# Deriving the feature map's derivative again in the backward instead of storing it, with a new order of the forward

## The chip, the core and the metric

The program runs on one core of one Trainium2 chip, in one launch. The metric is the device time of an execution in microseconds, the median of several. Before the change it is 2144.93 us (three runs, 2142.76 to 2145.81).

## The reference

Four attention blocks in a row over 2048 tokens of width 640 (32 heads of 20): a linear one (A), a sliding one (B, window 256), A and B again with the same weights; then the gradients of the result with respect to the input and the four weight matrices. All in bf16. The part that the change touches is the feature map phi of the linear block:

```python
x = x + _A_ref(_layernorm(x, axis=-1), A_wqkv, A_wo)
x = x + _B_ref(_layernorm(x, axis=-1), B_wqkv, B_wo)
...
phi = lambda t: jnp.where(t > 0, t + 1, jnp.exp(t)) + 1e-6
pq, pk = phi(q), phi(k)
kv = jnp.einsum("bhsd,bhse->bhde", pk, v)
z = jnp.einsum("bhsd->bhd", pk)
num = jnp.einsum("bhqd,bhde->bhqe", pq, kv)
den = jnp.einsum("bhqd,bhd->bhq", pq, z)[..., None] + 1e-6
```

Its derivative is 1 for t > 0 and exp(t) otherwise, that is min(exp(t), 1). Since phi is max(t, 0) + min(exp(t), 1) + 1e-6, the same derivative is also min(phi - 1e-6, 1).

## The kernel before

The tokens are cut into 16 tiles of 128. The layers have the numbers 0 (A), 1 (B), 2 (A), 3 (B). The span runs through five parts:

- a first pass over the tiles for layer 0 (`a_first`): layer norm, q, k and v, the feature map;
- a joined pass (`ab_pass(0)`) that finishes layer 0, does layer 1, and begins layer 2 (its k and v alone);
- a joined pass (`ab_pass(2)`) that finishes layer 2 and does layer 3, with the start of the backward;
- the sliding backward of layer 3 (`B_attn_bwd`), then a backward phase `bwd_phase(3, 2, 1)` for the projections of layer 3 and the linear block of layer 2;
- the same again for layers 1 and 0, `bwd_phase(1, 0, None)`, at the end of the span.

In the forward, q and k of a tile come out of PE in halves of 320 columns (`a_qkv`, line 488). For each half ACT writes the exponential into a buffer `ee` (line 516), DVE takes the minimum with 1 in place (line 517), and DVE adds max(t, 1e-6) to it and so writes phi (line 520), for q into `pp`, for k into the persistent `gcar`. Line 467 copies transposes of q's phi to `pqT` on ACT, and line 501 copies half of v out of PSUM on ACT in layer 0. ACT's queue then issues the stores of a tile (line 416): `pq` and `pk`, the feature maps, `eq` and `ek`, the derivatives, and `v`. `ee` is a ring of four buffers, and a buffer is free again when its store has landed. Layer 2's queries are done later, from the layer norm kept in `pqT` (`late_q`, line 542): for the first `EARLY` tiles as fillers between the two joined passes, for the others inside `ab_pass(2)`; matmuls are line 553, and `pq` and `eq` are stored from there.

In the second half of a backward phase `lin_grads` (line 1465) does a tile of the linear block's gradients. Its `start` flips dNT, pkT and vT by DMA transposes and loads `eq` and `ek` on SP's queue (line 1128), into rings of two buffers each. Six chunks follow; for q and k DVE multiplies what PE has summed by `eq` or `ek` (line 1503). `tail` (line 1276) then carries the result through the projection: ACT copies dh (line 1309), DVE forms a product and its sum (line 1317), ACT scales (1324), POOL adds the gradient so far (1327), DVE updates it (1329). In the first backward phase `local_dO` follows on the updated gradient: transposes, a projection, a product on POOL (1377), a reduction on DVE (1380), two small instructions on DVE (1382, 1384) and a store issued on ACT's queue (1387).

The order on each engine comes from a planner (`Sched`). Program code makes instructions in an order that the numbers in `AT` set for the forward: each is a position in tiles, relative to a tile's number, at which a step's items are put (`num`, `out`, `outb`, `qkv`, `lag`, `af` and so on). The planner then walks the engines by estimated durations and picks on each the ready instruction that can start first, and among these the one made first. PE may take an instruction at most `AHEAD` places ahead of the first one not yet taken. DMAs are estimated too, on one channel, so a DMA that goes changes the estimated times of what follows. Each engine executes its list in order.

Of the kernel before, what the change touches and what calls it, by code (L numbers as in the profile page):

```python
# [18 lines left out]
HPAD = 32  # L19
WIN = 256  # L20
LN_EPS = 1e-5
AHEAD = 19
IDLE = 300


# [177 lines left out]
class Kern:  # L203
    def __init__(self, ctx, tc, x0, A_wqkv, A_wo, B_wqkv, B_wo, grad_out, outs):
# [68 lines left out]
        for l in (0, 2):  # L273
            self.sv[l] = dict(
                pq=d.tile([T, D], BF, name=f"pq{l}"), pk=d.tile([T, D], BF, name=f"pk{l}"),
                eq=d.tile([T, D], BF, name=f"eq{l}"), ek=d.tile([T, D], BF, name=f"ek{l}"),
                v=d.tile([T, D], BF, name=f"v{l}"), o=d.tile([T, D], BF, name=f"o{l}"),
                r32=d.tile([T, self.H], F32, name=f"r32{l}"),
                mbd=d.tile([D, D + P], BF, name=f"mbd{l}"),
            )  # L280
# [53 lines left out]
    def forward(self, slabs):  # L334
# [5 lines left out]
        with ExitStack() as st:  # L340
# [147 lines left out]
            def a_qkv(l, tt, hnT):  # L488
# [3 lines left out]
                def chunk(ci):  # L492
                    def f():
# [27 lines left out]
                            out=pd(), in0=ps.t[:, 0:CW], scalar=1e-6, in1=es(), op0=ALU.max,  # L521
                            op1=ALU.add), [ps, (e, ci)], [(c["p"], ci) if kind == "q" else ("pk", tt, ci)])
                        if ci == 3 and "q" in c:
                            p_, e = c["p"], c["q"]
                            turn("s", lambda: pqT[:, :, tt * P:(tt + 1) * P], lambda: p_.t, DT, [(p_, 0), (p_, 1)],
                                 [("pqT", tt)])
                            dma("ACT", lambda: self.tm_view(sv["pq"])[:, tt, :], lambda: p_.t, 160 * KB,
                                [(p_, 0), (p_, 1)], [])
                            dma("ACT", lambda e=e: self.tm_view(sv["eq"])[:, tt, :], lambda e=e: e.t, 160 * KB,
                                [(e, 0), (e, 1)], [])  # L530
                        if ci == 3:
                            e = c["k"]
                            dma("ACT", lambda: self.tm_view(sv["pk"])[:, tt, :], lambda: pk[:, tt, :], 160 * KB,
                                [("pk", tt, 2), ("pk", tt, 3)], [])
                            dma("ACT", lambda e=e: self.tm_view(sv["ek"])[:, tt, :], lambda e=e: e.t, 160 * KB,
                                [(e, 2), (e, 3)], [])
                    return f
                return [chunk(ci) for ci in range(6)]

# [2 lines left out]
            def late_q(l, tt, where="s1", **F):  # L542

                sv = self.sv[l]
                q_left.discard(tt)
                e, p_ = R["ee"].buf(), R["pp"].buf()
                own = lambda: pqT[:, :, tt * P:(tt + 1) * P]
                for ci in range(2):
                    ps, c0 = R[where].buf(), ci * CW
                    for k0, k1 in ((0, 2), (2, DT)):  # L550
                        def f(ps=ps, c0=c0, k0=k0, k1=k1):
                            for k in range(k0, k1):
                                nc.tensor.matmul(ps.t[:, 0:CW], lhsT=own()[:, k, :], rhs=wsb["Wqkv_A"][:, k, c0:c0 + CW],
                                                 start=(k == 0), stop=(k == DT - 1))
                        op("PE", pe([CW] * (k1 - k0)), f, [("pqT", tt), ("Wqkv_A", ci)], [ps], **F)
                    es = lambda c0=c0: e.t[:, c0:c0 + CW]
                    op("ACT", av(CW), lambda ps=ps, es=es: nc.scalar.activation(es(), ps.t[:, 0:CW], ACT.Exp), [ps],
                       [(e, ci)], **F)
                    op("DVE", v4(CW), lambda es=es: nc.vector.tensor_scalar(out=es(), in0=es(), scalar1=1.0, scalar2=None,
                                                                            op0=ALU.min), [], [(e, ci)], **F)  # L560
                    op("DVE", vp(CW), lambda ps=ps, es=es, c0=c0: nc.vector.scalar_tensor_tensor(
                        out=p_.t[:, c0:c0 + CW], in0=ps.t[:, 0:CW], scalar=1e-6, in1=es(), op0=ALU.max, op1=ALU.add),
                       [ps, (e, ci)], [(p_, ci)], **F)
                if tt < 2:
                    turn("mm", own, lambda: p_.t, DT, [(p_, 0), (p_, 1)], [("pqT", tt)])
                else:
                    flip(own, lambda: p_.t, 160 * KB, [(p_, 0), (p_, 1)], [("pqT", tt)], **F)
                dma("ACT", lambda: self.tm_view(sv["pq"])[:, tt, :], lambda: p_.t, 160 * KB, [(p_, 0), (p_, 1)], [], **F)
                dma("ACT", lambda: self.tm_view(sv["eq"])[:, tt, :], lambda: e.t, 160 * KB, [(e, 0), (e, 1)], [], **F)

            def a_kv(l):
                sv = self.sv[l]
# [390 lines left out]
            def a_first(items, l, base, lag=0.0, late=()):  # L963


                for tt in range(TT):
# [10 lines left out]
                        return lambda: cell["fs"][i]()  # L977
                    spread(items, base + tt + 0.9 + lag, base + tt + 1.9 + lag, [g(i) for i in range(6)][2 * (tt in late):])

            EARLY = 6  # L980
            AT = {0: dict(num=-2.458, out=-1.707, outb=1.792, step=0.144, qkv=-0.99, wide=0.745, lag=0.42, af=2.042, al=-0.11),
                  2: dict(lq=-3.207, num=-2.403, out=-1.76, outb=1.696, step=0.086, qkv=-0.985, wide=0.584, lag=0.35, gT=0.745, dO=1.691, dOs=0.137)}

            def ab_pass(l, last):
                a = AT[l]
# [105 lines left out]
    def bwd_phase(self, lb, la, nb, ahead, raw):  # L1091
# [9 lines left out]
        with ExitStack() as st:  # L1101
# [363 lines left out]
            def lin_grads(tt, items, t0):  # L1465
# [4 lines left out]
                def start():  # L1470
                    for nm, src, size in (("dNT", self.tmp_dN, 192 * KB), ("pkT", sv["pk"], 160 * KB),
# [1 line left out]
                        c[nm] = b = R[nm].buf()  # L1473
                        flip(lambda b=b: b.t, lambda src=src: src[row, :], size,
                             [("dNd", tt)] if nm == "dNT" else [], [b])
                    c["eq"], c["ek"] = load("eq", sv["eq"], tt), load("ek", sv["ek"], tt)

                def chunk(kind, ci):
                    def f():
# [413 lines left out]
```

## Time and profile before

| | |
|---|---|
| median of the runs | 2144.93 us |
| the profiled execution, its own time | 2145.22 us |
| its span, first to last instruction | 2143.5 us |
| PE busy in the span | 2008.2 us, 94% |
| DVE busy | 1440.1 us, 67% |
| ACT busy | 1203.3 us, 56% |
| POOL busy | 879.4 us, 41% |
| mean granted TensorE clock | 0.975 |
| q and k exponentials of the first pass (line 516) | 12.9 to 115.8 us |
| products with eq and ek (line 1503), first phase | 1218.4 to 1359.0 us |
| the same, last phase | up to 2066.7 us |

A row of engine instructions gives the start and the duration in us, the engine, the line, what it writes and reads with partitions x elements, and in brackets how long the engine sat idle before it and what ended that. A row of stretches gives the busy us of PE, its weight loads, DVE, ACT and POOL with the number of instructions in brackets, the granted clock, the share of the DMA engines and GB/s. Rows with ACTq or SPq are DMA issues on an engine's queue; they aren't in the busy time. A row of one line's instructions has its count, and minimum, median and maximum in ns. A row that groups has, behind the bar, the busy us and the mean ns of one, then the idle time before them.

### The profile page before, as it was taken

How to read it: one execution, taken by the hardware profiler on the slowest of the kernel's cores; microseconds unless marked ns; L12 is line 12 of the kernel's file. 1: busy time of each engine (PE TensorE's matmuls, PEld its weight loads, DVE VectorE, ACT ScalarE, POOL GpSimd, SP SyncE). 2: the span in 40 equal slices, each digit the busy share in tenths (PEclk: the TensorE clock that was granted, in tenths of full speed). 3: DMA queues.
4: the chain of work that ended last, by engine and by line, in shares of the span. 5: the costliest groups of instructions: out<-in, count | busy, mean ns of one | idle time of the engine just before them, and what ended most of it. 6: DMA issues, size and time to landing. Idle time of an engine off the chain costs nothing. (4 is left out here: it accounts for less than half of the span.)

```text
span 2143.5 us, 68024 instructions
## 1 busy us (share of the span) xinstructions
PE 2008.2 (94%) x27908; PEld 1389.2 (65%) x27908; DVE 1440.1 (67%) x2954; ACT 1203.3 (56%) x1995; POOL 879.4 (41%) x1850
## 2 busy tenths in 40 slices
PE   6879999889999899999899999999999999999999
PEld 4656666656666577777666667656777765666764
DVE  6757777567776599999634368606998984444651
ACT  3527878647888589899422233216988881221430
POOL 1015666316777456666223223204665652230210
PEclk9989999999999899999899999999999999999999
DMA  9928989469998788987987899847999998989943
GB/s 291 256 106 179 191 193 191 119 198 201 210 208 191 146 157 151 161 161 155 193 185 168 213 200 203 175 104 142 157 158 151 170 170 162 199 185 227 186 111 102
DMA packets 943687, 376.43 MB, mean 176 GB/s; under 512 B 821776, under 2 KB 923664, under 8 KB 943120
## 3 DMA queue, kind: packets, MB, share of 16 engines
q1 hardware_dynamic: 866176, 299.16, 71.9%
q10 hardware_dynamic: 77200, 72.94, 11.1%
q8 instruction: 218, 3.57, 0.7%
q14 instruction: 93, 0.76, 0.1%
HBM read 109.02 MB, written 112.07 MB: 103 GB/s over the span
## 5 line engine op out<-in xcount | busy, mean ns | idle before, releaser
L1693 DVE TENSOR_TENSOR ds_sb<-pair,e_sb 128x768 bf16<-128x768 f32 x480 | 437.6, 951 | 57.8 <-PE pair L1654 49.6
L1673 ACT ACTIVATE e_sb<-pair 128x768 bf16<-128x768 f32 x480 | 390.9, 815 | 95.6 <-PE pair L1654 67.4
L839 POOL TENSOR_SCALAR_AFFINE_SELECT e_sb<-e_sb 128x384 bf16<-128x384 bf16 (+1 forms) x512 | 198.3, 406 | 357.5 <-ACT e_sb L830 335.7
L830 ACT ACTIVATE e_sb<-s_ps 128x1152 bf16<-128x1152 f32 (+2 forms) x256 | 273.8, 1070 | 100.2 <-PE s_ps L826 78.4
L1685 POOL TENSOR_SCALAR_AFFINE_SELECT e_sb<-e_sb 128x256 bf16<-128x256 bf16 x448 | 182.0, 406 | 227.1 <-ACT e_sb L1673 226.9
L1327 POOL TENSOR_TENSOR gw<-w,gcar 128x640 f32<-128x640 f32 x64 | 89.4, 1397 | 423.4 <-ACT w L1324 406.8
L1138 PEld LDWEIGHTS <-slabR 128*128 128x128 bf16 x1920 | 185.6, 98 | 116.1 <-DMA slabR<-o 3.7
L1682 POOL TENSOR_SCALAR_AFFINE_SELECT e_sb<-e_sb 128x256 bf16<-128x256 bf16 x512 | 206.5, 406 | 89.3 <-ACT e_sb L1673 89.3
L1718 PEld LDWEIGHTS <-dsT 128*128 128x128 bf16 x2880 | 146.2, 97 | 97.7 <-issue 91.5
L1709 ACT COPY dsT<-dsT_ps 128x768 bf16<-128x768 bf16 x240 | 191.2, 796 | 9.4 <-PE dsT_ps L1706 6.6
L448 PE MATMUL mm_ps<-slabR,hnTB 128*128 128x320 bf16 x960 | 170.5, 308 | 10.5 <-DVE gcar L520 6.0
L1706 PE MATMUL dsT_ps<-ident,ds_sb 128*128 128x128 bf16 x1848 | 158.2, 223 | 1.3 <-ACT dsT L1709 1.1
L1722 PEld LDWEIGHTS <-ds_sb 128*128 128x128 bf16 x2880 | 145.1, 96 | 0.8 <-issue 0.8
L1722 PEld LDWEIGHTS <-e_sb 128*128 128x128 bf16 x2880 | 145.0, 96 | 0.0
L844 POOL TENSOR_SCALAR_AFFINE_SELECT e_sb<-e_sb 128x512 bf16<-128x512 bf16 x224 | 142.6, 636 | 0.0
L833 ACT ACTIVATE e_sb<-s_ps 128x384 bf16<-128x384 f32 (+2 forms) x256 | 119.9, 468 | 32.3 <-PE s_ps L826 15.1
L1138 PE MATMUL dw_ps<-dqkv,slabR 128*128 128x480 bf16 x640 | 134.7, 366 | 0.0
L1309 ACT ACTIVATE dh<-mm_ps 128x320 f32<-128x320 f32 x64 | 28.0, 437 | 189.8 <-PE mm_ps L1138 164.9
L1138 PE MATMUL dw_ps<-dqkv,om 128*128 128x480 bf16 x640 | 134.2, 366 | 0.0
L1654 PE MATMUL pair<-slabR 32*128 32x384 bf16 (+2 forms) x1024 | 120.5, 326 | 12.0 <-DVE ds_sb L1693 5.2
L1138 PEld LDWEIGHTS <-om 128*128 128x128 bf16 x800 | 77.5, 98 | 71.3 <-DMA om<-o 2.4
L864 PEld LDWEIGHTS <-e_sb 128*128 128x128 bf16 x2880 | 105.5, 96 | 26.6 <-POOL e_sb L844 7.5
(234 smaller groups left out, 4357.6 us busy)
## 6 DMA issues: line engine op xcount, KB each, us to landing
qkvp<-qk_slab SPq DMA_DIRECT2D x64, 256.0 KB, 3.7
hn<-slabR SPq DMA_DIRECT2D x64, 160.0 KB, 2.9
qkvp<-v_slab SPq DMA_DIRECT2D x32, 256.0 KB, 3.4
slabR<-qkvp SPq DMA_DIRECT2D x16, 512.0 KB, 4.8
o<-o SPq DMA_DIRECT2D x48, 160.0 KB, 2.9
eq<-ee ACTq DMA_DIRECT2D x32, 160.0 KB, 3.0
pq<-pp ACTq DMA_DIRECT2D x32, 160.0 KB, 2.4
ek<-ee ACTq DMA_DIRECT2D x32, 160.0 KB, 2.7
```

The lines of the kernel that those rows point to most:

```text
L448: nc.tensor.matmul(ps.t[:, w0:w0 + width], lhsT=lhsT(), rhs=rhs(), start=start, stop=stop)
L830: op("ACT", av(3 * nkt * P), lambda: nc.scalar.activation(e.t[:, 0:3, 0:nkt, :], s3.t[:, :, 0:nkt * P].rearrange("p h (i q) -> p h i q", q=P),
L839: nc.gpsimd.affine_select(out=v, in_=v, compare_op=ALU.is_ge, fill=0.0, base=0, pattern=[[0, h1 - h0], [1, P]], channel_multiplier=-1)
L1138: nc.tensor.matmul(ps.t[:, w0:w0 + width], lhsT=lhsT(), rhs=rhs(), start=start, stop=stop)
L1673: nc.scalar.activation(E[n][:, 2 * p:2 * p + 2], PR[h][:, :, 0:3 * P].rearrange("p i (j q) -> p i j q", q=P), ACT.Exp, scale=self.c_att)
L1682: nc.gpsimd.affine_select(out=e[:, :, j, :], in_=e[:, :, j, :], compare_op=ALU.is_ge, fill=0.0, base=0, pattern=[[0, 2], [-1, P]], channel ...
L1685: nc.gpsimd.affine_select(out=e[:, :, j, :], in_=e[:, :, j, :], compare_op=ALU.is_ge, fill=0.0, base=-1, pattern=[[0, 2], [1, P]], channel ...
L1693: nc.vector.tensor_mul(DS[n][:, hs], PR.pop(h)[:, :, 0:3 * P].rearrange("p i (j q) -> p i j q", q=P), E[n][:, hs])
L1706: nc.tensor.transpose(ps[:, i, j, :], DS[n][:, 2 * p + i, j, :], self.ident)
L1709: (nc.scalar.copy if by == "A" else nc.vector.tensor_copy)(TSB[h], TPS.pop(h))
L1718: nc.tensor.matmul(a[:, 0, hh, :], lhsT=TSB[2 * n + hh // 2][:, hh % 2, j, :], rhs=ld[g]["K"][:, k, cs], start=(i == 0), stop=(i == len(dq ...
L1722: nc.tensor.matmul(a[:, 1 + x, hh, :], lhsT=src[n][:, hh, j, :], rhs=ld[g][rhs][:, q, cs], start=(i == 0), stop=(i == len(dkv) - 1))
```

## The change

The forward keeps `ee` on chip only for phi and stores neither `eq` nor `ek`: 64 stores of 160 KB less on ACT's queue, from two places in `a_qkv` and one in `late_q`, and four DRAM tensors less. The backward loads `pq` and `pk` into the same buffers as it loaded `eq` and `ek`, and DVE takes min(x - 1e-6, 1) in place, in one instruction behind each load. The numbers of the forward change: `AHEAD`, `EARLY`, and all of `AT`.

```diff
-AHEAD = 19
+AHEAD = 18
...
-                eq=d.tile([T, D], BF, name=f"eq{l}"), ek=d.tile([T, D], BF, name=f"ek{l}"),
...
                         if ci == 3 and "q" in c:
-                            p_, e = c["p"], c["q"]
+                            p_ = c["p"]
...
-                            dma("ACT", lambda e=e: self.tm_view(sv["eq"])[:, tt, :], lambda e=e: e.t, 160 * KB,
-                                [(e, 0), (e, 1)], [])
                         if ci == 3:
-                            e = c["k"]
...
-                            dma("ACT", lambda e=e: self.tm_view(sv["ek"])[:, tt, :], lambda e=e: e.t, 160 * KB,
-                                [(e, 2), (e, 3)], [])
...
-                dma("ACT", lambda: self.tm_view(sv["eq"])[:, tt, :], lambda: e.t, 160 * KB, [(e, 0), (e, 1)], [], **F)
...
-            EARLY = 6
-            AT = {0: dict(num=-2.458, out=-1.707, outb=1.792, step=0.144, qkv=-0.99, wide=0.745, lag=0.42, af=2.042, al=-0.11),
-                  2: dict(lq=-3.207, num=-2.403, out=-1.76, outb=1.696, step=0.086, qkv=-0.985, wide=0.584, lag=0.35, gT=0.745, dO=1.691, dOs=0.137)}
+            EARLY = 8
+            AT = {0: dict(num=-2.329, out=-1.53, outb=1.773, step=0.003, qkv=-0.851, wide=0.713, lag=0.391, af=2.216, al=-0.231),
+                  2: dict(lq=-3.14, num=-2.341, out=-1.768, outb=1.691, step=0.084, qkv=-0.988, wide=0.634, lag=0.313, gT=0.79, dO=1.598, dOs=0.307)}
...
-                    c["eq"], c["ek"] = load("eq", sv["eq"], tt), load("ek", sv["ek"], tt)
+                    for nm, p_ in (("eq", "pq"), ("ek", "pk")):
+                        c[nm] = b = load(nm, sv[p_], tt)
+                        op("DVE", 310, lambda b=b: nc.vector.tensor_scalar(
+                            out=b.t, in0=b.t, scalar1=-1e-6, scalar2=1.0, op0=ALU.add, op1=ALU.min), [], [b])
```

## The prediction

> **What bounds the kernel now.** I read first the page, then stretches of 50 us, then the instructions around what the change removes and adds.
>
> ```profile
> span 2143.5 us, 68024 instructions
> ```
>
> ```profile
> core 0: us, PE busy (x) PEld busy (x) DVE busy (x) ACT busy (x) POOL busy (x), PEclk, DMA share, GB/s
> ...
> 50.00:100.00 50.00, 43.39 (x394) 31.73 (x393) 37.73 (x108) 30.83 (x76) 0.00 (x0) 1.00 0.98 254
> ...
> 200.00:250.00 50.00, 47.49 (x821) 33.51 (x820) 38.64 (x97) 40.95 (x67) 32.94 (x73) 1.00 0.88 180
> ...
> 550.00:600.00 50.00, 49.11 (x851) 34.60 (x849) 39.40 (x98) 41.27 (x63) 37.70 (x78) 1.00 1.05 220
> ...
> 1300.00:1350.00 50.00, 47.26 (x440) 35.99 (x439) 44.46 (x96) 15.80 (x42) 16.19 (x12) 1.00 1.06 209
> ...
> 2000.00:2050.00 50.00, 50.00 (x510) 39.49 (x508) 35.90 (x87) 21.19 (x54) 11.18 (x8) 1.00 0.88 179
> ```
>
> Five stages matter. In the first pass over the tiles (row at 50 us) no engine is full and the DMA share is 0.98. In the two passes that join a linear and a sliding layer (200 and 550 us) PE is busy 95 and 98 per cent. In the second half of the first backward phase (1300 us) PE is at 95 and DVE at 89 per cent: the two wait for each other. In the same half of the last phase (2000 us) PE is never idle and DVE has 14.1 of 50 us free. Busy time leaves out the issuing of DMAs, and this is where the first pass is decided:
>
> ```profile
> L416 ACTq DMA_DIRECT2D eq<-ee x32: 326/422/1445, 15.0 to 654.7; - x32
> L416 ACTq DMA_DIRECT2D pq<-pp x32: 326/332/628, 15.5 to 654.4; - x32
> L416 ACTq DMA_DIRECT2D ek<-ee x32: 326/388/672, 23.6 to 422.8; - x32
> L416 ACTq DMA_DIRECT2D pk<-gcar x32: 339/345/1209, 25.5 to 423.3; - x32
> L416 ACTq DMA_DIRECT2D v<-vv x32: 338/363/972, 25.9 to 424.8; - x32
> ```
>
> These are the five stores of a tile (minimum, median, maximum ns): by their medians 0.422 + 0.332 + 0.388 + 0.345 + 0.363 = 1.85 us of ACT's queue. The period of a tile comes from the copy of a half of v, of which these are the first and the eleventh in a steady row:
>
> ```profile
> 53.47 0.42 ACT L501 CAST vv<-s_ps 128x320 bf16<-128x320 f32 x1 [0.47 <-PE s_ps L448]
> ...
> 113.28 0.42 ACT L501 CAST vv<-s_ps 128x320 bf16<-128x320 f32 x1 [0.98 <-DVE vv L504]
> ```
>
> (113.28 - 53.47) / 10 = 5.98 us. The 50 us of the row then hold 8.36 tiles, so a tile takes 5.19 us of PE, 4.51 of DVE and 3.69 of ACT; with the issues ACT's queue is taken for 5.54 of 5.98 us. One tile shows the harm:
>
> ```profile
> 68.45 0.69 ACT L467 COPY pqT<-s_ps 128x640 bf16<-128x640 bf16 x1
> 68.45 0.99 ACTq L416 DMA_DIRECT2D eq<-ee  x1
> ...
> 69.54 0.39 ACTq L416 DMA_DIRECT2D ek<-ee  x1
> ...
> 69.97 0.42 ACT L501 CAST vv<-s_ps 128x320 bf16<-128x320 f32 x1 [0.83 <-PE mm_ps L448]
> ...
> 70.44 0.84 PE L448 MATMUL s_ps<-Wqkv_A,hnTA 128*128 128x320 bf16 x5 [0.68 <-ACT vv L501]
> ```
>
> The copy starts 0.04 us after ek's issue has ended, 0.83 us after ACT's last work, and PE stands 0.68 us until it has its bank back.
>
> **The change part by part.** *Stores in the first pass.* eq and ek of 16 tiles go, 0.81 us of the queue per tile. The gain lies between nothing (another engine sets the same period) and 16 x (5.98 - 5.19) = 12.6 us, where PE sets it. I take the store that stands right ahead of the copy, ek: 16 x 0.388 = **6.2 us gained**.
>
> *Stores in the two joined passes.* There go 16 of ek (layer 2's keys) and 16 of eq (its queries, recomputed late): 16 x 0.388 + 16 x 0.422 = 13.0 us of ACT's queue. But there ACT waits for PE:
>
> ```profile
> ACT e_sb L830 <- PE s_ps L826: 46.0, 55, 12.7
> ```
>
> 46.0 us in 55 waits between 120 and 420 us. Between 0 and 13.0 I take a quarter, **3 us gained**.
>
> *EARLY from 6 to 8.* Two more tiles' late queries run as fillers between the passes and not inside the second one. The row groups the matmuls of the ten tiles that run inside it; the second row is where the fillers go:
>
> ```profile
> L553 PE MATMUL mm_ps<-Wqkv_A,pqT 128*128 128x320 bf16 x100 | 16.7, 298 | 0.0
> ```
>
> ```profile
> 440.00:450.00 10.00, 8.05 (x85) 5.82 (x82) 7.53 (x22) 4.96 (x10) 0.00 (x0) 1.00 1.06 268
> ```
>
> A tile takes 1.67 us of PE; two leave a stage with PE at 98 per cent for one with 1.95 of 10 us free. Between 3.3 us gained and 3.3 lost (the fillers delay the sums that the next pass waits for), I take **2 us gained**.
>
> *New positions and AHEAD 18.* They change the order of the same instructions. Nothing in the rows prices an order. PE is idle 2.51 of 50 us at 200 us, so over some 410 us of joined passes 20 us; I let a quarter of that, 5 us, go either way and take **0**.
>
> *Recomputation.* Each backward phase now reads pq and pk where it read eq and ek: as many loads on SP, of the same size, with no queue moved. Behind each load stands one DVE instruction, in place on 128x640 bf16; 64 in all. Its duration isn't in the trace. The same operation on half the length and another on the same length:
>
> ```profile
> L517 DVE TENSOR_SCALAR ee<-ee x96: 225/234/686, 13.4 to 422.5; 128x320 bf16<-128x320 bf16 x96
> ```
>
> ```profile
> L482 DVE TENSOR_SCALAR slabR<-x,mv,rs x64: 430/446/774, 9.3 to 678.6; 128x640 bf16<-128x640 bf16 x64
> ```
>
> Between 0.234 and 0.446 I take the middle, 0.34 us: 0.68 per tile, 10.9 us in a phase of 16 tiles. The instruction also waits for its load, of which this is the row of the DMA issues (KB, median us to landing):
>
> ```profile
> eq<-eq SPq DMA_DIRECT2D x32, 160.0 KB, 3.4
> ```
>
> Behind the waiting instruction would stand all of DVE's evacuations and behind these PE. The loads are issued about a tile ahead (two buffers), so I price this wait at nothing; without that lead it is up to 3.4 us for a load.
>
> In the last phase the work goes into DVE's free time: a tile's 0.68 against 14.1 us per 50. PE covers it without a gap, so **0**; with the cover gone it would be 10.9. In the first phase there is a closed chain:
>
> ```profile
> 1293.64 1.34 POOL L1377 TENSOR_TENSOR prod<-slab,o 128x640 f32<-128x640 bf16 x1
> 1293.72 1.95 DVE L1329 SCALAR_TENSOR_TENSOR gcar<-slabR,sm,gw 128x640 bf16<-128x640 bf16 x1 [0.35 <-POOL gw L1327]
> ...
> 1295.99 0.80 DVE L1380 TENSOR_REDUCE dd<-prod 128x32 f32<-128x640 f32 x1
> ...
> 1297.10 0.30 DVE L1384 SCALAR_TENSOR_TENSOR slab<-dd,slab 128x32 bf16<-128x32 f32 x1
> ...
> 1297.43 0.37 ACTq L1128 DMA_DIRECT2D dOpt<-slab  x1
> ...
> 1297.85 0.44 ACT L1309 ACTIVATE dh<-dw_ps 128x320 f32<-128x320 f32 x1 [2.01 <-DVE dqkv L1503]
> ...
> 1298.41 0.82 DVE L1317 CUSTOM_DVE_ANT_0 scr<-dh,slabR 128x640 bf16<-128x640 f32 x1 [0.30 <-ACT dh L1309]
> ...
> 1299.49 0.92 ACT L1324 ACTIVATE w<-dh,sm,rs 128x640 f32<-128x640 f32 x1 [0.18 <-DVE sm L1323]
> ...
> 1300.49 1.40 POOL L1327 TENSOR_TENSOR gw<-w,gcar 128x640 f32<-128x640 f32 x1 [5.50 <-ACT w L1324]
> ...
> 1301.92 1.95 DVE L1329 SCALAR_TENSOR_TENSOR gcar<-slabR,sm,gw 128x640 bf16<-128x640 bf16 x1 [0.35 <-POOL gw L1327]
> ```
>
> From the gradient's update on DVE through the reduction, ACT's store, ACT's copy, DVE's product, ACT, POOL and back to the update: 1301.92 - 1293.72 = 8.20 us, the period of a tile. (ACT's copy of dh names a product on DVE as its releaser, but starts 0.05 us after the store's issue has ended, and that issue stands ahead of it in ACT's queue.) DVE waits twice in it, 0.30 and 0.35 us. A new instruction put into one of these gaps costs next to nothing; one put between the update and the store lengthens the chain by all of its 0.34. Between 0 and 16 x 0.68 = 10.9 us I take half, **5.4 us lost**; the update, and with it the transposes on PE that read it, are then what comes late.
>
> The sum: -6.2 - 3 - 2 + 0 + 5.4 = -5.8 us. The profiled execution took 2145.22 us (1.7 outside its span); that gives 2139.4. It stands 0.3 above the median of the runs, 2144.93, so the forecast is **2139.1 us**.
>
> **The rivals.** *The chain in the first backward phase takes it back.* If both instructions stand between the update and the store, the whole 10.9 us counts. There is more: an instruction of this kind is held while POOL works.
>
> ```profile
> 273.17 0.63 POOL L844 TENSOR_SCALAR_AFFINE_SELECT e_sb<-e_sb 128x512 bf16<-128x512 bf16 x1
> 273.21 0.69 DVE L517 TENSOR_SCALAR ee<-ee 128x320 bf16<-128x320 bf16 x1 [1.36 <-ACT ee L516]
> ```
>
> POOL ends at 273.80, DVE's instruction at 273.90, after 0.69 us where its median is 0.234. In the chain POOL works for 2.74 of 8.20 us. With half of the 32 instructions held for 0.45 us (0.686 - 0.234) it is 7.2 us more. Forward's 11.2 us gained, 18.1 lost: 2145.2 + 6.9, less 0.3, is 2151.8 us, slower. It decides once the period exceeds 8.20 + 11.2 / 16 = 8.9 us. For it speaks DVE's 89 per cent, against it the two gaps, which hold 0.65 of the 0.68.
>
> The Trainium skill, SBUF — State Buffer, "Who interferes with whom", states the same as a rule: a DVE instruction in a two-port mode and a GpSimd instruction exclude each other, whoever comes second waits until the first has ended. By that rule alone a new instruction that comes just behind POOL's sum waits for nearly all of it, three times the hold that I priced; the pair above agrees with it.
>
> *What goes is hidden anyway.* The five stores are only what ACT does while PE is busy, the period of the first pass stays near PE's and DVE's own chain, and the backward's work lies in its gaps: forward gains 2, the backward loses 2, 2144.9 us. For it speaks that many of ACT's waits in the first pass name PE; against it, that PE waited for ACT in the tile shown.
>
> *The whole bound comes.* First pass 12.6, half of 13.0 in the joined passes, 3.3 from EARLY, nothing lost behind: -22.4, 2122.5 us. It asks that PE run without a gap from the first tile on, while at 50 us it still loses 6.6 of 50.
>
> **How the numbers follow.** About 0.2 per cent, 4.3 us, is what a measurement tells from no change. The forecast gets 0.45 (own range 2131 to 2145: 0.33 of it faster, 0.12 within the bound), the lengthened chain 0.23 (0.21 slower, 0.02 within), the hidden work 0.20 (0.16 within, 0.02 to each side), the whole bound 0.12. Faster 0.47, same 0.30, slower 0.23. The range 2127 to 2154 leaves out most of the whole bound's case and the tail of the lengthened chain.
>
> **What would show it.** In the first pass the eq and ek issues are gone and the copy of v follows ACT's last work; the period falls from 5.98 to about 5.6 us. The second joined pass has eight instead of ten late tiles. In the first backward phase the update's period grows from 8.20 to about 8.5 us, and the new instruction takes 0.3 to 0.4 us, more where POOL runs. In the last phase PE stays without a gap. The prediction is wrong if the first pass keeps its period, if the chain's period passes 8.9 us, if DVE stands waiting for pq or pk, or if the new order opens gaps in the joined passes.

## The result and the profile after

The changed kernel takes **2125.76 us** (median of 4 runs, 2123.76 to 2129.68), the kernel before, run beside it, 2143.85 us (4 runs, 2141.27 to 2145.81). The ratio is 0.9923, 95% interval 0.9909 to 0.9937: 16.5 us by the ratio. The forecast was 2139.1 us. The sign was right, but the gain is about three times the 5.8 us forecast. The median of the runs lies 1.2 us below the range of 2127 to 2154 us; the ratio applied to 2144.93 us, from which the forecast started, gives 2128.4, just inside it.

The line of the page with the span, after:

```profile
span 2122.0 us, 67891 instructions
```

The two profiled spans are 21.5 us apart (2143.5 and 2122.0). Landmarks, read from the first or last row of a line in each trace, cut the difference up (us):

| stretch | before | after | difference |
|---|---|---|---|
| start to the last copy of v on ACT (first pass) | 117.8 | 104.4 | -13.4 |
| from there to the last exponential of layer 2's keys (first joined pass) | 304.0 | 296.2 | -7.8 |
| from there to the first product of layer 3's sliding backward (second joined pass, seams) | 316.8 | 312.8 | -4.0 |
| first to last product of that sliding backward | 307.1 | 310.0 | +2.9 |
| first to last update of the gradient, first backward phase | 318.1 | 318.3 | +0.2 |
| the sliding backward of layer 1 | 307.9 | 306.0 | -1.9 |
| first to last update of the last phase | 295.0 | 296.9 | +1.9 |
| all seams and the end | 176.8 | 177.4 | +0.6 |

The whole gain lies in the forward, and more than half of it in the first pass. The two rows of the sliding backward are code that the change does not touch; over all kernels of this study the first of them took 305.4 to 314.3 us, so a difference of 2 or 3 us in one stretch of one profile means nothing by itself.

Part of the 21.5 us is not the change. PE is idle for 135.3 us of the span before and 119.0 after, 16.3 us less; the other 5.2 us are shorter busy time (2008.2 and 2003.0 us) for the same number of matmul records (27908). The mean granted TensorE clock was 0.975 in the one profile and 0.981 in the other, and it varies between executions of one kernel (0.976 to 0.983 in 31 runs of the kernel before). The 16.3 us agree with the 16.5 of the ratio. By the first three rows of the table PE's idle time falls by 10.6, 7.5 and 1.3 us, and in the rest of the span it grows by 3.1.

The same five stretches of 50 us as in the prediction, after (columns as there: busy us of PE, its weight loads, DVE, ACT, POOL with counts, granted clock, DMA share, GB/s):

```profile
core 0: us, PE busy (x) PEld busy (x) DVE busy (x) ACT busy (x) POOL busy (x), PEclk, DMA share, GB/s
50.00:100.00 50.00, 48.54 (x461) 36.26 (x459) 38.82 (x115) 34.81 (x81) 0.00 (x0) 1.00 0.90 224
200.00:250.00 50.00, 49.48 (x848) 35.05 (x846) 41.05 (x100) 41.60 (x69) 34.09 (x75) 1.00 0.92 183
550.00:600.00 50.00, 48.66 (x829) 33.98 (x830) 37.71 (x95) 40.58 (x62) 37.44 (x78) 1.00 0.93 199
1300.00:1350.00 50.00, 48.69 (x426) 35.60 (x425) 45.07 (x102) 16.19 (x41) 16.20 (x12) 1.00 0.96 188
2000.00:2050.00 50.00, 49.74 (x503) 39.18 (x501) 37.02 (x92) 20.16 (x53) 11.12 (x8) 1.00 0.72 142
```

In the first pass PE now works 48.54 of 50 us where it worked 43.39, in the first joined pass 49.48 where it worked 47.49. Late in both backward phases it is about as full as it was, with more work on DVE.

The first pass in the instructions of ACT, after: the copy of a half of v, the first and the tenth in a steady row.

```profile
51.80 0.42 ACT L500 CAST vv<-s_ps 128x320 bf16<-128x320 f32 x1
...
98.98 0.42 ACT L500 CAST vv<-s_ps 128x320 bf16<-128x320 f32 x1
```

A tile takes (98.98 - 51.80) / 9 = 5.24 us, down from 5.98, and so comes close to the 5.19 us that the prediction had worked out for PE's own work. Inside one tile, after:

```profile
67.65 0.84 PE L447 MATMUL s_ps<-Wqkv_A,hnTA 128*128 128x320 bf16 x5
67.85 0.69 ACT L466 COPY pqT<-s_ps 128x640 bf16<-128x640 bf16 x1 [0.64 <-PE s_ps L463]
...
68.53 0.43 ACT L500 CAST vv<-s_ps 128x320 bf16<-128x320 f32 x1
...
68.80 0.34 ACTq L415 DMA_DIRECT2D pk<-gcar  x1
69.01 0.84 PE L447 MATMUL s_ps<-Wqkv_A,hnTA 128*128 128x320 bf16 x5
```

The copy starts at 68.53, where the copy of the transposes ends; before, two issues stood between them. PE goes on at 69.01 without the wait of 0.68 us.

The first backward phase in the order of time, after: the chain from one update of the gradient to the next.

```profile
1289.10 1.94 DVE L1322 SCALAR_TENSOR_TENSOR gcar<-slabR,sm,gw 128x640 bf16<-128x640 bf16 x1 [0.35 <-POOL gw L1320]
...
1290.96 0.31 DVE L1471 TENSOR_SCALAR slabR<-slabR 128x640 bf16<-128x640 bf16 x1
1291.20 0.81 DVE L1373 TENSOR_REDUCE dd<-prod 128x32 f32<-128x640 f32 x1
...
1292.64 0.34 ACTq L1121 DMA_DIRECT2D dOpt<-slab  x1
...
1293.24 0.32 DVE L1471 TENSOR_SCALAR eq<-eq 128x640 bf16<-128x640 bf16 x1
...
1293.87 0.82 DVE L1310 CUSTOM_DVE_ANT_0 scr<-dh,slabR 128x640 bf16<-128x640 f32 x1
...
1297.37 1.95 DVE L1322 SCALAR_TENSOR_TENSOR gcar<-slabR,sm,gw 128x640 bf16<-128x640 bf16 x1 [0.35 <-POOL gw L1320]
```

The period is 1297.37 - 1289.10 = 8.27 us (8.20 before). The keys' instruction does stand between the update and the store, but the distance from the update to the reduction is 2.10 us (1291.20 - 1289.10), where the prediction's rows gave 2.27 (1295.99 - 1293.72): other work on DVE moved behind the store to make room. The queries' instruction stands where DVE used to wait 0.30 us ahead of `scr`; that product now has no wait ahead of it.

The rows of the new instruction (count, minimum, median, maximum in ns, first and last start), and what its engine waited for ahead of it, after:

```profile
L1471 DVE TENSOR_SCALAR eq<-eq x32: 314/319/602, 1044.2 to 2036.0; 128x640 bf16<-128x640 bf16 x32
L1471 DVE TENSOR_SCALAR slabR<-slabR x16: 311/314/983, 1044.5 to 1332.4; 128x640 bf16<-128x640 bf16 x16
L1471 DVE TENSOR_SCALAR ek<-ek x16: 318/327/1517, 1771.7 to 2036.2; 128x640 bf16<-128x640 bf16 x16
...
  DMA ek<-pk: 13.2, 11
  DMA eq<-pq: 4.4, 4
```

The median is 0.31 to 0.33 us, and DVE stood 17.6 us in 15 waits for the loads.

### The profile page after: what moved, and what is told of

It is laid out like the page before. It is cut to its first block, busy times and chain, and to the rows that moved or that the text cites. A ratio compares the mean times of both kernels' runs of the same rounds, so it can differ in the third digit from the quotient of the medians.

```text
span 2122.0 us, 67891 instructions
## 1 busy us (share of the span) xinstructions
PE 2003.0 (94%) x27908; PEld 1384.9 (65%) x27908; DVE 1456.4 (69%) x3018; ACT 1204.6 (57%) x1995; POOL 878.8 (41%) x1850
## 5 line engine op out<-in xcount | busy, mean ns | idle before, releaser
L857 PE MATMUL pv_ps<-v_slab,e_sb 128*128 128x32 bf16 x2880 | 121.1, 177 | 6.0 <-POOL e_sb L837 5.2
```

Of the source, the lines that this page charges most:

```text
L857: nc.tensor.matmul(pv.t[:, h % 16, :], lhsT=e.t[:, hh, j, :], rhs=vts[j].t[:, h, :], start=(j == 0), stop=(j == nkt - 1))
```

## The experiments

Three questions: what the stores cost in the first pass, what the recomputation costs, and what the new order does. Each kernel was run beside the kernel before on the same chip, and that kernel gave medians of 2142.24, 2140.98 and 2142.6 us in the three groups of runs. The stretches are those of the table above.

| kernel | time, us | ratio to before, 95% | first pass | first joined pass | second, with seams | updates, first phase | updates, last phase |
|---|---|---|---|---|---|---|---|
| before | 2143.85 | | 117.8 | 304.0 | 316.8 | 318.1 | 295.0 |
| after | 2125.76 | 0.9923, 0.9909 to 0.9937 | 104.4 | 296.2 | 312.8 | 318.3 | 296.9 |
| layer0_only | 2136.24 | 0.9967, 0.9954 to 0.9980 | 105.4 | 306.2 | 316.0 | 316.7 | 297.3 |
| stores_on_sp | 2144.45 | 1.0015, 0.9999 to 1.0030 | 110.3 | 307.9 | 317.9 | 317.1 | 295.5 |
| small_stores | 2146.84 | 1.0023, 1.0008 to 1.0038 | 119.4 | 302.2 | 314.4 | 320.4 | 296.7 |
| recompute_only | 2140.68 | 1.0000, 0.9983 to 1.0016 | 118.7 | 302.4 | 316.2 | 319.1 | 297.5 |
| drop_oldpos | 2143.5 | 1.0010, 0.9990 to 1.0030 | 104.3 | 317.6 | 313.7 | 317.8 | 296.7 |
| keep_newpos | 2142.44 | 0.9995, 0.9975 to 1.0014 | 117.7 | 300.2 | 316.8 | 319.3 | 295.2 |
| after_early6 | 2128.4 | 0.9936, 0.9912 to 0.9960 | 104.6 | 297.6 | 311.7 | 318.3 | 298.3 |
| recompute_twice | 2142.98 | 1.0003, 0.9984 to 1.0022 | 104.1 | 296.4 | 311.4 | 336.1 | 298.1 |
| old_at0 | 2151.84 | 1.0046, 1.0023 to 1.0070 | 105.4 | 316.5 | 314.0 | 319.0 | 299.1 |
| old_at2 | 2131.25 | 0.9946, 0.9929 to 0.9964 | 104.4 | 298.6 | 314.5 | 317.6 | 299.6 |
| ahead19 | 2125.6 | 0.9921, 0.9897 to 0.9945 | 103.8 | 296.7 | 312.1 | 319.5 | 299.2 |
| fused | 2122.58 | 0.9908, 0.9881 to 0.9934 | 104.3 | 298.1 | 310.4 | 318.2 | 295.4 |

### The stores of the first pass

*layer0_only*: the kernel before, with layer 0's two stores dropped and the derivative recomputed in the last phase; layer 2, and all positions, as before.

```diff
-                            dma("ACT", lambda e=e: self.tm_view(sv["eq"])[:, tt, :], lambda e=e: e.t, 160 * KB,
-                                [(e, 0), (e, 1)], [])
...
+                            if l:
                                 dma("ACT", lambda e=e: self.tm_view(sv["ek"])[:, tt, :], lambda e=e: e.t, 160 * KB,
...
+                    if la:
+                        c["eq"], c["ek"] = load("eq", sv["eq"], tt), load("ek", sv["ek"], tt)
+                        return
```

> The kernel before; eq and ek of layer 0 alone are no longer stored, and the last phase recomputes them. Layer 2 and all positions stay as before. Theory (the stores of the first pass account for its gain, whatever the positions): the last copy of v in the first pass moves from 117.8 to 103 to 108 us, and the kernel takes 9 to 14 us less than before. Rival (the first pass is faster only because of AHEAD 18 and a new order): the copy stays at 115 or later and the kernel is within 4 us of before.

The first pass ends at 105.4 us, 12.4 earlier, with the old positions. This is the cleanest measure of the stores of the first pass. The time falls by 6.0 us by the medians (2136.24 beside 2142.24) and 7 by the ratio, short of the 9 to 14 expected: the first joined pass takes 2.2 us more and the updates of the last phase 2.3.

*stores_on_sp*: the same two stores kept, issued on SP's queue.

```diff
-                            dma("ACT", lambda e=e: self.tm_view(sv["eq"])[:, tt, :], lambda e=e: e.t, 160 * KB,
+                            dma("SP", lambda e=e: self.tm_view(sv["eq"])[:, tt, :], lambda e=e: e.t, 160 * KB,
...
-                            dma("ACT", lambda e=e: self.tm_view(sv["ek"])[:, tt, :], lambda e=e: e.t, 160 * KB,
+                            dma("SP" if l == 0 else "ACT", lambda e=e: self.tm_view(sv["ek"])[:, tt, :], lambda e=e: e.t, 160 * KB,
```

> The kernel before; in the first pass the 32 stores of eq and ek are issued on SP's queue and not on ACT's. The traffic is the same and the buffers are held as long or longer. Theory (the time of ACT's queue is what the stores cost): the last copy of v moves from 117.8 to 110 us or earlier. Rival (what counts is the traffic on the DMA engines, or the buffer that is free only when its store has landed): it stays at 116 or later.

The pass ends at 110.3 us, 7.5 of the 13.4 us earlier and a little past the 110 expected. Not all of the 7.5 can be put down to ACT's queue: over the first 50 us the granted clock was 0.90 before and 0.97 here. From 50 to 100 us, with the clock at 1.00 in both, PE works 44.29 us of 50, little more than the 43.39 before; in layer0_only it works 47.99. Before, 5.7 us of PE's waits between 48 and 110 us were for work that ACT began within 0.15 us of the end of an issue. Here none is, yet PE waits 8.1 us in all where it waited 9.0.

```profile
50.00:100.00 50.00, 44.29 (x378) 31.83 (x376) 37.29 (x109) 32.16 (x80) 0.00 (x0) 1.00 1.05 264
```

The waits between 30 and 118 us (total us, times, longest) show PE and ACT still handing a bank to and fro there:

```profile
ACT vv L501 <- PE s_ps L448: 7.7, 9, 1.0
PE s_ps L448 <- ACT vv L501: 6.4, 10, 1.7
```

Whether the order or the buffers that wait for their stores keep it there was not separated; against the buffers speaks that the trace names the landing of an `eq` store only once in this pass as what an exponential of ACT waits for, 0.5 us. The next pass takes 3.9 us more, with no more idle time of PE than before (28.9 us in both) but a lower granted clock (0.95 beside 0.96). Where layer 3's backward begins 2.5 us of the 7.5 are left (736.1 beside 738.6), and the median of the runs is not below that of before.

*small_stores*: as layer0_only, but in place of each dropped store one of 32 of the 640 columns: as many issues, a twentieth of the bytes.

```diff
+                            dma("ACT", lambda e=e: self.tm_view(sv["eq"])[:, tt, 0:32], lambda e=e: e.t[:, 0:32], 8 * KB,
...
+                                dma("ACT", lambda e=e: self.tm_view(sv["ek"])[:, tt, 0:32], lambda e=e: e.t[:, 0:32], 8 * KB,
```

> As the kernel in which layer 0 alone is recomputed, but with 32 stores put back on ACT's queue in the old places, each of the first 32 of 640 columns: as many issues as before, a twentieth of the bytes. What they write is read by nobody. Theory (issue time): the last copy of v stays at 114 us or later. Rival (traffic): it comes at 103 to 108 us as without the stores. In between, both count, and the share is read from where it lies.

The pass ends at 119.4 us, no earlier than with the whole stores. Its granted clock is 0.94 there beside 0.96 before, which by an estimate (0.02 of 119 us) hides 2 us at most of the 12. The rows of these issues before, up to 110 us, and in this kernel, up to 112:

```profile
L416 ACTq DMA_DIRECT2D eq<-ee x15: 326/333/989, 15.0 to 109.8; - x15
L416 ACTq DMA_DIRECT2D ek<-ee x14: 326/350/672, 23.6 to 106.5; - x14
```

```profile
L416 ACTq DMA_DIRECT2D eq<-ee x15: 332/333/445, 14.3 to 110.8; - x15
L416 ACTq DMA_DIRECT2D ek<-ee x14: 326/344/443, 22.9 to 107.1; - x14
```

By the medians a store of 8 KB holds ACT's queue for as long as one of 160 KB, and the pass gains nothing from the bytes. So in the first pass the price of a store is not its traffic. Its place in ACT's queue is part of the price, as the tile of the prediction and the waits counted above show; how much of the 12.4 us it makes is not shown.

### The recomputation

*recompute_only*: the kernel before, all stores kept, with the loads and the new instruction of the change in the backward.

```diff
-                    c["eq"], c["ek"] = load("eq", sv["eq"], tt), load("ek", sv["ek"], tt)
+                    for nm, p_ in (("eq", "pq"), ("ek", "pk")):
+                        c[nm] = b = load(nm, sv[p_], tt)
+                        op("DVE", 310, lambda b=b: nc.vector.tensor_scalar(
+                            out=b.t, in0=b.t, scalar1=-1e-6, scalar2=1.0, op0=ALU.add, op1=ALU.min), [], [b])
```

> The kernel before with the new backward alone: the forward still stores eq and ek, at the old positions, but the backward loads pq and pk and recomputes. Theory (the planner puts the new instructions where the chain of the first backward phase has room): 0 to 3 us slower than before, the update's period in the first backward phase 8.2 to 8.35 us. Rival of the prediction (half of the new work lies on the chain): 5 us slower, the period near 8.5 us.

The ratio is 1.0000 (0.9983 to 1.0016). The updates of the first phase take 1.0 us more, those of the last 2.5. The first number is within what one stretch varies. The second is not: over the table the updates of the last phase take 295.0 to 295.5 us in the four kernels without the instruction there (before, stores_on_sp, keep_newpos, fused) and 296.7 to 299.6 in the ten with it. The time is added where the linear block's tiles begin: from the sixteenth update to the seventeenth it is 46.3 to 46.8 us in the four and 47.7 to 51.0 in the ten. From there to the last update the changed kernel takes no longer than the one before (98.0 and 98.4).

*recompute_twice*: the changed kernel with a second DVE instruction of the same shape behind each new one (adds 0, takes the minimum with 1 again).

```diff
+                        op("DVE", 310, lambda b=b: nc.vector.tensor_scalar(
+                            out=b.t, in0=b.t, scalar1=0.0, scalar2=1.0, op0=ALU.add, op1=ALU.min), [], [b])
```

> The changed kernel with a second DVE instruction of the same kind behind each recomputation (adding 0, minimum with 1, which changes no value): 64 more of 0.32 us. In the first backward phase the 16 tiles' updates stretch over 318.3 us from the first of the phase to its last, in the changed kernel and before (318.1). Theory (the first instruction went into gaps of 0.65 us a tile, and these are now used up): the stretch grows by 5 to 10 us, the period there from 8.27 to 8.6 to 8.9 us, and the last phase by at most 2 us. Rival (the chain through ACT and POOL has more room than that): the stretch grows by less than 2 us.

The same work once more costs all of the gain: 2142.98 us. The updates of the first phase take 17.8 us more than in the changed kernel, far beyond the 5 to 10 expected, the last phase only 1.2. The stretch from 1300 us shows how (row of that kernel):

```profile
1300.00:1350.00 50.00, 42.07 (x393) 31.77 (x392) 47.29 (x105) 14.41 (x38) 15.01 (x11) 1.00 0.82 163
```

PE falls from 48.69 to 42.07 us while DVE rises to 47.29 of 50: DVE now sets the pace. 17.8 us is more than the added 16 x 2 x 0.32 = 10.2, so the first instruction had used up the gaps and the second pushes the chain back by its full length and more. Why it is more was not looked into.

*fused*: the changed kernel without the new instruction. The product itself takes min(phi, 1) times PE's sum; this leaves out the subtraction of 1e-6.

```diff
-                            op("DVE", dve_ns(CW), lambda: nc.vector.tensor_mul(dst(), ps.t[:, 0:CW], e.t[:, e0:e0 + CW]),
+                            op("DVE", dve_ns(CW), lambda: nc.vector.scalar_tensor_tensor(
+                                out=dst(), in0=e.t[:, e0:e0 + CW], scalar=1.0, in1=ps.t[:, 0:CW], op0=ALU.min, op1=ALU.mult),
```

> The changed kernel without the new instruction: the product takes the minimum itself, min(phi, 1) times PE's sum, in one instruction of DVE per half. This leaves out the subtraction of 1e-6. Theory (the recomputation costs 1 us in the first backward phase and 2 in the last): 2 to 3 us faster than the changed kernel, 2123 us, with the stretch of updates at 316 to 318 us in the first phase and 295 in the last. Rival: the new form of the product takes longer on DVE than the plain product and sits in the chain, so that nothing is gained or some us are lost (2126 to 2132 us).

It has the lowest median of all kernels here, 2122.58 us, 3.0 below ahead19, which ran beside it and is the changed kernel but for one constant. The product takes as long as it did; the row of the fused kernel, and below it that of the changed one (ns, first backward phase):

```profile
L1497 DVE SCALAR_TENSOR_TENSOR dqkv<-eq,mm_ps x32: 474/477/489, 1194.6 to 1330.0; 128x320 bf16<-128x320 bf16 x32
```

```profile
L1499 DVE TENSOR_TENSOR dqkv<-mm_ps,eq x32: 476/481/493, 1196.5 to 1333.9; 128x320 bf16<-128x320 f32 x32
```

Minimum and product in one instruction cost what the product cost alone. The updates of the first phase take the same 318 us, though the median period in their second half is 8.17 us beside 8.28, and those of the last take 1.5 less, so most of what is left of the recomputation's price is in the last phase. The intervals of the two ratios overlap, and the 3 us are not beyond doubt.

### The order

*drop_oldpos*: the change without its new numbers: AHEAD 19, EARLY 6, both lines of AT as before.

```diff
-AHEAD = 18
+AHEAD = 19
...
-            EARLY = 8
-            AT = {0: dict(num=-2.329, out=-1.53, outb=1.773, step=0.003, qkv=-0.851, wide=0.713, lag=0.391, af=2.216, al=-0.231),
...
+            EARLY = 6
+            AT = {0: dict(num=-2.458, out=-1.707, outb=1.792, step=0.144, qkv=-0.99, wide=0.745, lag=0.42, af=2.042, al=-0.11),
...
```

> The changed kernel with AHEAD 19, EARLY 6 and the positions of before: all 64 stores are dropped and recomputed. In its profile the start of the sliding backward (the first product with the weights) was at 738.6 us before and is at 713.4 us in the changed kernel; the kernel that drops layer 0's stores alone has 727.6. Theory (the first pass gives about 11 us and the new positions most of the rest): it starts at 723 to 729 us, the kernel is 6 to 10 us faster than before. Rival (the joined passes gain by the stores that go there, whatever the positions): it starts at 713 to 718 us, 15 us or more faster.

Neither expectation held. The first pass ends at 104.3 us, as early as in the changed kernel, and the first joined pass then takes 317.6 us, 13.6 more than before the change: PE is idle 6.7 us longer there (35.6 and 28.9), and busy 6.8 us longer, at a granted clock of 0.95 beside 0.96. The ratio is 1.0010: dropping the stores alone gives nothing.

*keep_newpos*: the reverse, the kernel before with the new numbers.

```diff
-AHEAD = 19
+AHEAD = 18
...
-            EARLY = 6
-            AT = {0: dict(num=-2.458, out=-1.707, outb=1.792, step=0.144, qkv=-0.99, wide=0.745, lag=0.42, af=2.042, al=-0.11),
...
+            EARLY = 8
+            AT = {0: dict(num=-2.329, out=-1.53, outb=1.773, step=0.003, qkv=-0.851, wide=0.713, lag=0.391, af=2.216, al=-0.231),
...
```

> The kernel before with AHEAD 18, EARLY 8 and the new positions: all stores kept, the backward untouched. Theory (the new order is worth some 10 us by itself): the first pass ends as before (last copy of v near 118 us), the sliding backward starts at 725 to 731 instead of 738.6 us, the kernel is 6 to 12 us faster. Rival (the positions fit only the program without the stores): it starts at 736 us or later, no change or slower.

The first joined pass takes 3.8 us less, and PE is idle 4.3 us less in it (24.6 and 28.9). The sliding backward starts at 734.7 us, between the two expectations, and the time does not move. Alone, each half of the change is worth nothing that can be measured; together they are worth 16.5 us.

*old_at0*, *old_at2*, *ahead19*, *after_early6*: the changed kernel with one of the new numbers put back: the line of AT for the first joined pass, that for the second, AHEAD, EARLY.

```diff
-            AT = {0: dict(num=-2.329, out=-1.53, outb=1.773, step=0.003, qkv=-0.851, wide=0.713, lag=0.391, af=2.216, al=-0.231),
+            AT = {0: dict(num=-2.458, out=-1.707, outb=1.792, step=0.144, qkv=-0.99, wide=0.745, lag=0.42, af=2.042, al=-0.11),
```

> Only the positions of the first joined pass (the line AT[0]) go back to those of before; stores dropped, AHEAD 18, EARLY 8 and AT[2] as in the changed kernel. Theory (the gain stands or falls with an order of the first joined pass that fits the instructions without the stores): the first pass ends as early as in the changed kernel (last copy of v at about 104 us), then the joined pass takes some 310 to 320 us to the last exponential of layer 2's keys instead of 296, and the time is 2138 to 2148 us, 12 to 22 above the changed kernel. Rival (the order of the second joined pass, or AHEAD, carries it): 296 to 300 us for the first joined pass, and at most 5 us above the changed kernel.

```diff
-                  2: dict(lq=-3.14, num=-2.341, out=-1.768, outb=1.691, step=0.084, qkv=-0.988, wide=0.634, lag=0.313, gT=0.79, dO=1.598, dOs=0.307)}
+                  2: dict(lq=-3.207, num=-2.403, out=-1.76, outb=1.696, step=0.086, qkv=-0.985, wide=0.584, lag=0.35, gT=0.745, dO=1.691, dOs=0.137)}
```

> Only the positions of the second joined pass (the line AT[2]) go back to those of before. Theory: the first joined pass is untouched (last exponential at 400 to 402 us), and the second, in which only 8 stores less are issued inside, changes by 0 to 6 us: 2126 to 2132 us. Rival (each pass needs its own new order): the second joined pass loses 10 us or more, 2136 us or later.

```diff
-AHEAD = 18
+AHEAD = 19
```

> The changed kernel with AHEAD 19 as before, nothing else. The theory that any move of the planner's choices spoils the fitted order expects a first joined pass that is 5 to 20 us longer and 2131 to 2146 us; the rival, that one place more or less changes few choices of PE, expects the same landmarks within 3 us and 2124 to 2129 us.

```diff
-            EARLY = 8
+            EARLY = 6
```

> The changed kernel with EARLY 6: two more tiles have their late queries inside the second joined pass. Theory (a tile is worth its 1.67 us of PE, moved from a full stage to one with gaps): the sliding backward starts 2 to 4 us later than 713.4 us. Rival (the fillers delay the sums, so EARLY gives nothing): it starts within 1.5 us of it, or earlier.

It is the first joined pass: with its old positions it takes 316.5 us, and the time is 2151.84, slower than before the change and 3.8 us beyond the range expected. With the second line put back the median is 5.5 us higher (2131.25 beside 2125.76, inside the theory's range), but the intervals of the two ratios overlap, its own pass takes 1.7 us more, and the profile has a granted clock of 0.974 beside 0.981; PE is idle 120.9 us in its span beside 119.0. So a gain from that line is not shown. AHEAD and EARLY give nothing that can be told, as their rivals expected.

Of the 20.3 us by which the pass is longer than after, 15.3 are idle time of PE (36.7 and 21.4), and 4.9 are busy time at a lower granted clock (0.96 beside 0.97). What goes wrong is seen in the waits between 118 and 402 us. Before:

```profile
DVE qk_slab L695 <- PE mm_ps L448: 17.9, 38, 1.4
...
PE s_ps L826 <- ACT e_sb L830: 3.6, 8, 1.3
```

After:

```profile
DVE qk_slab L688 <- PE mm_ps L447: 7.1, 16, 0.9
...
PE s_ps L819 <- ACT e_sb L823: 1.9, 4, 1.0
```

With the old positions of this pass (old_at0):

```profile
DVE qk_slab L688 <- PE mm_ps L447: 31.0, 34, 2.8
...
PE s_ps L819 <- ACT e_sb L823: 13.1, 15, 2.2
```

PE stands 13.1 us until ACT has taken an exponential out of the bank that the next scores need, seven times as long as after; DVE in turn stands 31.0 us for PE. One of the longest of these stalls, in the order of time, old_at0:

```profile
234.74 0.49 ACT L826 ACTIVATE e_sb<-s_ps 128x384 bf16<-128x384 f32 x1
...
234.90 0.49 DVE L519 SCALAR_TENSOR_TENSOR gcar<-mm_ps,ee 128x320 bf16<-128x320 f32 x1
...
235.43 0.41 ACTq L415 DMA_DIRECT2D pk<-gcar  x1
...
235.87 1.87 ACTq L415 DMA_DIRECT2D o<-oB  x1
...
237.78 0.46 ACTq L415 DMA_DIRECT2D linv<-slabR  x1
...
238.34 1.13 ACT L823 ACTIVATE e_sb<-s_ps 128x1152 bf16<-128x1152 f32 x1 [3.11 <-DVE vv L503]
...
239.53 0.35 PE L819 MATMUL s_ps<-QT,KT 32*128 32x128 bf16 x12 [2.02 <-ACT e_sb L823]
```

ACT is done at 235.23, and the first of three stores behind it waits until DVE has written pk at 235.39. The three then stand in a row in ACT's queue ahead of the exponential: 0.41 + 1.87 + 0.46 = 2.74 of the 3.11 us in which ACT has no work. PE stands 2.02 us for the bank behind it. The bracket names a copy of v on DVE as the releaser, but ACT's queue tells another story: the exponential follows the last issue by 0.10 us. The same three stores stand ahead of the exponential in ten of the 15 waits, once for a tile from 203 to 363 us, and these ten make 10.9 of the 13.1 us. In drop_oldpos there are ten as well, 10.8 us; before and after there is none with the three. Before, two of the three stood between single exponentials:

```profile
228.80 0.33 ACTq L416 DMA_DIRECT2D o<-oB  x1
...
228.98 1.13 ACT L830 ACTIVATE e_sb<-s_ps 128x1152 bf16<-128x1152 f32 x1
...
230.25 0.33 ACTq L416 DMA_DIRECT2D linv<-slabR  x1
...
230.85 1.13 ACT L830 ACTIVATE e_sb<-s_ps 128x1152 bf16<-128x1152 f32 x1 [0.36 <-PE s_ps L826]
```

This is the harm that the prediction saw in the first pass, now made by the order. Between before and drop_oldpos the order of ACT's own 355 instructions in this pass differs in four; what moved are the issues among them.

## Why the prediction came out as it did

**First pass: -6.2 forecast, -13.4 measured.** The direction was right, the size was half. The step that failed is "I take the store that stands right ahead of the copy, ek": it let one of the two issues count. Without the stores the pass falls onto PE, which is what the other end of the bound, 12.6, said (12.4 in layer0_only). The period is 5.24 us where the forecast was 5.6 and PE's bound 5.19. Freeing ACT's queue alone gave 7.5 us at most, so the queue does not account for all of it, and what else a store costs there stays open.

**Joined passes: -3 forecast for the issues, -11.8 measured with all that changed there.** The term was worked from ACT's queue, and there the change brought nothing. Added up row by row, from 7 us behind the last copy of v to 7 us ahead of the last exponential, the issues on ACT's queue in the first joined pass take 37.4 us in 104 issues before and 37.4 us in 91 after: thirteen fewer issues, and others became longer. Of the 11.8 us, 8.8 are idle time of PE; 7.5 of them are in the first joined pass, where old_at0 shows that the new order counts. In the second pass a gain of the forecast's size can be seen: its stretch takes 310.4 to 314.5 us in the eight kernels without the late stores (after, drop_oldpos and the six made from the changed kernel), 314.4 to 317.9 in those that keep them. The granted clock differs between these profiles too, but PE's idle time in the stretch shows the same: 19.2 to 21.9 us in the eight, 22.8 to 24.8 in the six.

**New positions: 0 forecast, with 5 us either way.** This is the step that failed outright: "PE is idle 2.51 of 50 us at 200 us, so over some 410 us of joined passes 20 us; I let a quarter of that, 5 us, go either way". It asked what the new order could be worth in the old program. That is the 3.8 us of keep_newpos. But dropping the stores had already changed the order, the issues of ACT's queue above all; the likely way is the planner's estimated times, which move when a DMA goes. Under the old positions the pass became 13.6 us longer, and with the new ones it is 7.8 shorter than before. In the changed program the positions carry 316.5 - 296.2 = 20.3 us in this one pass, 15.3 of them idle time of PE. The sum treated parts as additive that are not.

**EARLY: -2 forecast, nothing measured.** after_early6 has a ratio of 0.9936 (0.9912 to 0.9960) where the change has 0.9923, and its stretch of the second pass is 1.1 us shorter.

**Recomputation: +5.4 and 0 forecast, +0.2 and +1.9 measured**, and +1.0 and +2.5 in recompute_only. The duration was right (0.34 taken, 0.31 to 0.33 measured). The half of 10.9 us that should have stood on the chain was too much: both instructions fit into the gaps that the prediction had shown, and a product moved to make room. That the room ends there is shown by recompute_twice. The last phase was forecast as free and was not. DVE did stand waiting for the loads, which the prediction had priced at nothing and named as a sign of being wrong; with 17.6 us of waits the cost still stayed near 2 us. The 2 us lie where the linear block's tiles begin, and six of the waits, 7.0 us, lie there as well, between 1945 and 1965 us; that they are the cause is not shown.

**The lengthened chain** did not come: the period is 8.27 us, far from the 8.9 at which it decides. Its second half, the hold by POOL, is real and rare. These are the worst case of the new instruction and its neighbour on POOL, after:

```profile
1777.65 1.40 POOL L1411 TENSOR_TENSOR prod<-slabR,o 128x640 f32<-128x640 bf16 x1 [3.40 <-DVE slabR L1404]
1777.72 1.52 DVE L1471 TENSOR_SCALAR ek<-ek 128x640 bf16<-128x640 bf16 x1
```

POOL ends at 1779.05 and DVE at 1779.24. Of 64 instructions three last over 0.4 us (0.60, 0.98 and 1.52), and each ends 0.18 or 0.19 us behind a POOL instruction; the rival had 16 of 32 held in the first phase, and there it was one. The Trainium skill, SBUF — State Buffer, "Who interferes with whom", says that the one who comes second is blocked for the whole instruction of the other, and the three agree, at 1.5 us for the one that came 0.07 us behind POOL. So the rule held for DVE as the second, and the two seldom meet here. For POOL as the second these runs do not show it: two POOL instructions that began while a new one ran took 1.41 and 1.40 us, as long as others of their kind.

**The whole bound**, 2122.5 us, came nearest, in part by luck. Its term for the first pass, 12.6, was right; its 6.5 us from ACT's queue and 3.3 from EARLY were not what filled the rest.

## What to carry to other kernels

Where DMA issues stand in an engine's queue ahead of work that another engine waits for, price the whole group, not the last one: here dropping two stores a tile brought the pass down to the bound of the next full engine, and shrinking them to a twentieth of the bytes brought nothing. An order fitted to a program is part of the program: a change that drops or adds instructions has to be judged with positions found anew, because under the old ones it can look worthless (here 1.0010 where 0.9923 was to be had). In the closed chain of the first backward phase the gaps took new work for next to nothing until they were full; the same work again cost more than its own length.

## What the runs showed of the hardware that was not expected

The time that an issue holds ACT's queue varies widely and not with its size. These rows are of stores in the first joined pass (ns, minimum, median, maximum). After:

```profile
L415 ACTq DMA_DIRECT2D o<-oB x16: 326/329/360, 152.0 to 389.9; - x16
L415 ACTq DMA_DIRECT2D linv<-slabR x16: 326/536/1379, 152.3 to 389.3; - x16
```

With the old positions of that pass (old_at0):

```profile
L415 ACTq DMA_DIRECT2D o<-oB x15: 326/444/2051, 154.7 to 393.2; - x15
L415 ACTq DMA_DIRECT2D linv<-slabR x15: 326/479/623, 154.2 to 393.7; - x15
```

The store of `o` takes up to 0.36 us in the one order and up to 2.05 in the other, that of `linv` up to 1.38 and 0.62; what makes one long was not found.

Executions of one and the same kernel spread further than the prediction assumed when it took 0.2 per cent as what can be told: 31 runs of the kernel before lay between 2133.35 and 2147.38 us, 0.65 per cent apart. The spread goes with the granted clock: the twelve runs at 0.977 or less have a median of 2143.4 us, the nine at 0.980 or more one of 2140.0, and the fastest run has one of the two highest clocks, 0.983. Differences of 2 or 3 us between kernels of this study rest on the stretches, not on the times, and in a stretch PE's idle time is the safer measure, since its busy time moves with the clock (282.0 us in the first joined pass of drop_oldpos at 0.95, 274.9 after at 0.97).
